# A second table of turns, engines and buffer slots for the same 1,612 operations of an attention and long-convolution kernel

## The chip, the cores and the metric

One Trainium2 chip, one core. The metric is the time of one execution on the device in microseconds; the median of three runs stands for the kernel.

## The reference, cut to what matters

Two independent halves write the left and the right 576 columns of one output of 2048 rows.

```python
# A: 32 heads of 18, 4 segments of 512 rows, with a memory carried from segment to segment
q, k, v = x @ wq, x @ wk, x @ wv
for s in range(4):
    p = softmax(qs @ ks.T * scale + causal_mask)          # 512 x 512 for each head
    a_mem = (phi(qs) @ M) / (phi(qs) @ z + 1e-6)          # phi(t) = t+1 if t>0 else exp(t)
    o = g * a_mem + (1 - g) * (p @ vs)
    M, z = M + phi(ks).T @ vs, z + phi(ks).sum()
a = concat(o) @ wo
# B: a short filter of 4 taps, a product, a convolution over all 2048 rows by FFT, a product
kv = short_filter(k, shift_k) * v
y = irfft(rfft(kv) * rfft(ssm_k))[:2048] + kv * ssm_D
b = q * y
out = concatenate([a, b])
```

## The kernel before

The kernel builds a graph of 1,612 operations and then emits them in one written order. An operation is a small group of instructions on one engine: five matmuls into one PSUM tile, the copy of that tile to SBUF, one DMA. `ORDER` is that order. Each operation has three characters in it: two digits to the base of 64 give its number in the graph, and a letter gives its engine (P TensorE, A ScalarE, D VectorE, G GpSimd, S the queue of SyncE, which issues every DMA). Each engine runs its own operations strictly in this order, and a DMA whose data is not ready holds up all DMAs behind it. `PLACES` gives each of 1,039 buffers its slot; a slot is used again only when the last reader of the buffer before has ended. PSUM has eight banks (`ps1` takes one, `ps2` two).

```python
for i in range(0, len(order), 3):
    o = g.ops[64 * code[order[i]] + code[order[i + 1]]]
    o.eng = {"P": "PE", "A": "ACT", "D": "DVE", "G": "POOL", "S": "SP"}[order[i + 2]]
...
for o in order:
    o.fn(o.eng)
```

Half A, for each segment `s` (lines from 780 on): `x` loads five transposed tiles of the input (`xT`, L800); `qk` and `v` project them (PE, L150), `qkp` does so for the first two groups of heads of segment 0 in another layout; the copies `eqk`, `ev` go to `dn` and `V`; `qd` writes q and k to a scratch in DRAM and `pad` reads them back with each head on 32 partitions; `s0`, `s1`, `s2` are the scores of four heads in three pieces (PE, L1046), each followed by two exponentials of 128x1024 on ACT (`exs`, L1053) and a mask on POOL (`m`, L1060); `av` multiplies by V (L152), `eav` copies it, `ad` writes it to DRAM, `cs` and `am` read sums and rows back, `rs`, `rx`, `rsb`, `o` normalise, `num` and `oo` add the memory's part, `out` is the last projection, `eout` its copy, `oA` its store. `phe`, `phm`, `pha` make phi (exponential on ACT L889, maximum, minimum), and `tk` transposes it by DMA.

Half B, for five groups of 128 (the last 64) channels: `kT`, `vT` load k and v transposed (L374, L377), `dg` makes diagonal weights, `conv` is the short filter (PE), `kv` its product with v (DVE L404), `tinx` a 32x32 transpose (DVE L416); `xsh` loads the long filter, `dadd` adds D to it (needs the DMA `Dt`, L350); `F1x`, `F1h`, `F2x`, `F2h` are the two stages of a Fourier transform as matmuls (L152) with copies; `Q`, `P`, `Yi`, `Yr` multiply the spectra (DVE or POOL); `inv`, the transposing DMA `zt`, and `last` transform back; `y` multiplies by q; `yo` stores.

The tables of the Fourier transform are made on the chip: `iota` (POOL), `idx` (DVE, L288 and L290), `sin` (ACT, L295) for four quarters of `Ft`, and `w1iota`, `w1idx`, `w1sin`, `w1mask` for `W1`; `gT` (PE) and `g` turn `Ft` over for the inverse, `psie`, `psiT`, `psi` make a small matrix from `W1`. `beta` loads the gate, `gexp` takes its exponential (ACT L664). The sine and the exponential are in different activation tables, so each change from one to the other on ACT brings an ACT_TABLE_LOAD. Copies on ACT bring none.

Of the kernel before, what the change touches and what calls it, by code (L numbers as in the profile page):

```python
# [18 lines left out]
S = 2048  # L19
# [103 lines left out]
class Prog:  # L123
# [1159 lines left out]


ORDER = (
    "0RG00G01D06G09D0ZS0WS0-S0+S11S0VG0qG0YG0vG0zS10S0mG0oG0XS0aS0US0bG0wG0AA02G03D0pD1MD0cS14P1CP18P0tS0dS1wP16P1yP12P0rS"
    "0yS0TS0hS04A19A0iSGoS0xSGpS0SS0jS1RG15A1kAGqG1UP28PGvP17A07D1xD13D1zD1DA08A1hA0gS05G0BG1oD0ED26P1APGtP1PPGrP1iD1jD1VD"
    "29D2AS0FA0kA0CD0DA1nA27A0fSGuD1BDGWSGwD1WSGsDGxPGyDGzD1XSIDS1QA1SP22P23A0nG0GGIiGGXD1pD1TD0PP0LP0NP1lG1NPICS0QA0OAGkP"
    "GiPGaP1OAGlA0MA20P24P25AGjAGbD1mD2BSGePGgPGmPGhDH4PHAPGYPH8PGnAGcPH0PHBAGZAH1A21AH5DGfD2CSIOSIgS0sS1bS1YSG+PHCPH6PH9A"
    "GdD1+PG-DH7DHDDHkPHiPHEPHVPH2PHGP1KPHHDHlAH3AHWAHTPHZPHjAHaDHXPHKPHxP1LAHYA1tAHyAHLAI1P0HPHIPHUDHbG1uD0IDHJD1vDHFAHMD"  # L1290
    "HcDIPD1GP1EPI2D1HA1qA1FA1-A1IP2QPIaPISPIcP1JA2SAHmPIbD4bS4aS4dS4cS4ZSHnAIWPIePH-P1aS2ESIhS1cSIdDITDI0AIXA0JPIQPIUPHzP"
    "HdG1rG0KD1sDIYP2RAH+AIRAIfDIVD2TGHND2IPHoPHpDHqDHrDHODIjPIZAHtDHPD2JA2KA2XP4gP2YA2ZA2aG2MPHsD0lD2NA2OA5dPHeG4hD5eA4eP"
    "JcP4fD5DD2LG2bP5fP59A5CAJdD5gD5ED4iP4jD2dA2cA2PGKGS2eG4yS0uS1ZS1dS2DSIkD5JD5IA5KD5ADIlP2qP2rA2sAHQPHRDImDHSDJNPHfP2fP"
    "HhDI3GI5G5BDKHDI4DJOA2iPHgAHuP2UPHvDI6D2kA2VA2gAIpPHwA2jAInPIqDIoDI7PI8DI9A2xPIBSIAS2yAIrD2zA4kP2mPJ6P2WS1gS1eS2oA2nA"
# [45 lines left out]


# [63 lines left out]
```

## Time and profile before

| | us |
|---|---|
| three runs | 342.86, 340.09, 337.14 |
| median | 340.09 |
| the profiled execution | 341.92 |
| its span, first to last instruction | 340.2 |

| engine | busy us | share of the span |
|---|---|---|
| PE | 285.5 | 84% |
| DVE | 266.1 | 78% |
| ACT | 258.6 | 76% |
| POOL | 181.3 | 53% |

Busy times of PE come from modelled ends of pipelined matmuls. The mean granted clock of PE is 0.909 of full speed.

### The profile page before, as it was taken

The page shows a single profiled execution, that of the slowest core. Times are in us where ns is not written, and L with a number is a line of the kernel's source. Part 1 is how long each engine was busy: PE and PEld are TensorE (multiplying, and loading weights), DVE is VectorE, ACT ScalarE, POOL GpSimd, SP SyncE. Part 2 cuts the span into 40 slices and gives each one's busy share as a digit, 9 for nine tenths or more (in the row PEclk, how much of TensorE's full clock was granted, in tenths as well). Part 3 has the DMA queues.
Part 4 walks back from the last instruction along what each step waited for, and adds up shares of the span by engine and source line. Part 5 has one row for each costly group of instructions (what it writes and reads, how often), then busy time and mean ns, then how long its engine had stood idle before and what let it go on. Part 6 is the DMA issues. An engine that isn't in the chain of part 4 may idle for free.

```text
span 340.2 us, 8802 instructions
## 1 busy us (share of the span) xinstructions
PE 285.5 (84%) x3515; PEld 163.9 (48%) x3515; DVE 266.1 (78%) x454; ACT 258.6 (76%) x362; POOL 181.3 (53%) x228
## 2 busy tenths in 40 slices
PE   0886998889979868889998999989895788997776
PEld 0453575444744446444555556546453254453334
DVE  6557477898999998969889998889969965655670
ACT  2197787987977869837999986888689569879813
POOL 8694007282785975654437423794858742435600
PEclk9999799997998979959999999999998559579969
DMA  8687489791996964776689687757359347453204
GB/s 199 172 178 104 108 111 161 136 176 33 212 175 182 167 154 89 160 139 184 136 180 151 156 166 149 148 144 180 85 129 195 88 94 166 96 140 102 80 17 101
DMA packets 119011, 47.13 MB, mean 139 GB/s; under 512 B 101946, under 2 KB 112570, under 8 KB 118970
## 3 DMA queue, kind: packets, MB, share of 16 engines
q1 hardware_dynamic: 118970, 46.58, 67.1%
q8 instruction: 27, 0.44, 0.5%
q14 instruction: 14, 0.11, 0.1%
HBM read 17.74 MB, written 14.42 MB: 95 GB/s over the span
## 4 chain that ended last, share of the span: by engine, by line
PE 36%; DVE 25%; ACT 12%; DMA 9%; issue 6%; SPq 6%; POOL 4%; DVEq 0%; ACTq 0%; POOLq 0%
PE PS L150 20%; PE PS L152 12%; ACT P L1053 8%; PE PS L1046 4%; DVE A L158 4%; DMA a_scratch<-ou 3%; DMA pad<-qk_scratch 2%; DVE X L158 2%; SPq L800 2%; DVE T L520 2%; DMA Dt<-in_A_beta_dram 2%; DMA q<-in_B_q_dram 2%; DVE H L524 2%; DVE X L404 2%; DVE H L158 1%
## 5 line engine op out<-in xcount | busy, mean ns | idle before, releaser
L1053 ACT ACTIVATE P<-PS 128x1024 bf16<-128x1024 f32 x160 | 154.7, 1036 | 28.6 <-PE PS L1046 25.4
L1060 POOL TENSOR_SCALAR_AFFINE_SELECT P<-P 128x512 bf16<-128x512 bf16 (+1 forms) x112 | 81.0, 744 | 86.0 <-ACT P L1053 55.2
L1046 PE MATMUL PS<-pad 18*128 18x384 bf16 (+3 forms) x512 | 39.9, 323 | 12.9 <-ACT P L1053 5.9
L158 DVE CAST A<-PS 128x512 bf16<-128x512 f32 (+1 forms) x64 | 41.4, 680 | 9.6 <-PE PS L152 9.4
L150 PE MATMUL PS<-xT,wk 128*126 128x512 bf16 (+1 forms) x100 | 28.5, 423 | 11.1 <-DMA xT<-in_A_x_dram 9.6
L152 PEld LDWEIGHTS <-Ft 128*64 128x64 bf16 x704 | 24.7, 113 | 15.4 <-issue 11.7
L520 POOL TENSOR_TENSOR T<-X,H 128x512 bf16<-128x512 bf16 x16 | 20.0, 1271 | 21.4 <-DVE H L158 19.8
L156 ACT CAST A<-PS 128x512 bf16<-128x512 f32 (+1 forms) x48 | 26.8, 601 | 5.8 <-PE PS L152 5.7
L1046 PEld LDWEIGHTS <-pad 18*128 18x128 bf16 x512 | 12.4, 93 | 37.6 <-issue 33.7
L152 PE MATMUL PS<-P,V 128*32 128x256 bf16 (+3 forms) x512 | 26.2, 333 | 3.4 <-DVE A L158 1.7
L152 PE MATMUL PS<-W,xs 128*64 128x128 bf16 (+1 forms) x608 | 24.4, 225 | 5.0 <-DVE ou L158 1.6
L152 PE MATMUL PS<-A,Ft 128*64 128x128 bf16 (+1 forms) x640 | 25.8, 218 | 3.3 <-DVE ou L158 1.9
L150 PE MATMUL PS<-wo,am 126*128 126x288 bf16 (+1 forms) x152 | 26.6, 312 | 0.9 <-DVE am L1215 0.5
L152 PEld LDWEIGHTS <-xs 128*64 128x64 bf16 (+1 forms) x608 | 19.9, 114 | 12.4 <-issue 9.7
L150 PE MATMUL PS<-xT,wq 128*126 128x512 bf16 (+1 forms) x100 | 25.0, 382 | 0.0
L150 PE MATMUL PS<-wv,xT 128*128 128x288 bf16 x160 | 24.3, 294 | 0.5 <-ACT P L1053 0.5
L150 PEld LDWEIGHTS <-wk 128*126 128x126 bf16 (+1 forms) x100 | 13.5, 144 | 20.9 <-issue 8.5
L150 PE MATMUL PS<-X,dg 128*128 128x512 bf16 x80 | 21.6, 404 | 0.9 <-DMA X<-in_B_k_dram 0.9
L152 PEld LDWEIGHTS <-V 128*32 128x32 bf16 x512 | 12.4, 103 | 18.2 <-issue 9.2
L150 PEld LDWEIGHTS <-am 126*128 126x128 bf16 (+1 forms) x152 | 14.7, 105 | 9.8 <-issue 3.5
L158 DVE CAST dn<-PS 126x512 bf16<-126x512 f32 (+1 forms) x22 | 14.9, 682 | 5.4 <-PE PS L150 4.4
L150 PEld LDWEIGHTS <-xT 128*128 128x128 bf16 x160 | 15.1, 101 | 8.1 <-issue 3.0
(164 smaller groups left out, 555.4 us busy)
## 6 DMA issues: line engine op xcount, KB each, us to landing
pad<-qk_scratch SPq DMA_DIRECT2D x30, 256.0 KB
qk_scratch<-dn SPq DMA_DIRECT2D x16, 252.0 KB
a_scratch<-ou SPq DMA_DIRECT2D x31, 128.0 KB
out_dram<-oA SPq DMA_DIRECT2D x16, 144.0 KB
xs<-in_B_ssm_k_dram SPq DMA_DIRECT2D x4, 512.0 KB
q<-in_B_q_dram SPq DMA_DIRECT2D x8, 256.0 KB
out_dram<-q SPq DMA_DIRECT2D x8, 256.0 KB
am<-a_scratch SPq DMA_DIRECT2D x16, 126.0 KB
```

The lines of the kernel that those rows point to most:

```text
L150: self.nc.tensor.matmul(out, lhsT=lhsT, rhs=rhs, start=start, stop=stop)
L152: self.nc.tensor.matmul(out, lhsT=lhsT, rhs=rhs, start=start, stop=stop, tile_position=pos)
L156: self.nc.scalar.copy(out=out, in_=in_)
L158: self.nc.vector.tensor_copy(out=out, in_=in_)
L404: self.nc.vector.tensor_tensor(out=v, in0=self.psf(pc)[lo:P, :], in1=v, op=ALU.mult)
L520: eng.tensor_tensor(out=t[:, 512 * r:512 * r + 512], in0=x[:, 512 * r:512 * r + 512], in1=h[:, 512 - 512 * r:1024 - 512 * r], op=ALU.mult)
L524: eng.tensor_tensor(out=self.t(Ht)[:], in0=self.t(Xt)[:], in1=self.t(Ht)[:], op=ALU.mult)
L800: self.nc.sync.dma_start_transpose(out=self.t(b)[:], in_=self.A_x[0, L * s:L * s + L, c0:c0 + P])
L1046: nc.tensor.matmul(o, lhsT=t[r, 1, q0:q0 + P], rhs=t[r, 0, q0:L], start=True, stop=True, tile_position=(32 * j, 0))
L1053: self.nc.scalar.activation(out=out2(jj), in_=self.psf(pso[jj]), func=ACT.Exp, scale=scale)
L1060: self.nc.gpsimd.affine_select(out=ap, in_=ap, compare_op=ALU.is_ge, fill=0.0, base=0, pattern=pat + [[1, P]], channel_multiplier=-1)
```

## The change

The operations, their code and the buffers' sizes stay. `ORDER` and `PLACES` are replaced as a whole, so turns, engines and slots are new.

```diff
 ORDER = (
-    "0RG00G01D06G09D0ZS0WS0-S0+S11S0VG0qG0YG0vG0zS10S0mG0oG0XS0aS0US0bG0wG0AA02G03D0pD1MD0cS14P1CP18P0tS0dS1wP16P1yP12P0rS"
...
+    "0YG00G01D0oG02G0pD03D0cS0+S0-S11S10S0bG0qG06G04A05G0VG0RG0GG0HP07D08A0ID09D0BG0wG0zS0dS0ZS0iS0aS0US0XS0WS0TS1MG1RG0vG"
...
 PLACES = (
-    "101101164624031042600221314025504101221072312301101101100503132020610042646402635142546230602040461004650431160520424"
...
+    "010010006462040132703014021724115123121011203210100101001110630224006002450402432004404271060642061000454632146264406"
...
```

Read back into names, the first turns of each queue are these:

```
ACT before  sin01 w1sin eqk eqk phe eqk eqk sin00 phe sin11 gexp sin10 phe ev eqkp ev g10 g11 ...
ACT after   w1sin sin00 sin01 ev sin10 eqk phe eqk sin11 phe gexp eqk g10 g11 phe ev ...
DVE before  cols idx01 w1idx cmask wp0 idx00 ev eqk ev phm idx11 phm pha eqkp ev idx10 kv0.1 ...
DVE after   cols cmask w1idx idx00 psi idx01 idx10 dg0 ev ev idx11 phm eqk eqk pha eqk kv0.3 ...
SP  before  wk wq x(5) wq4 wk4 sk4 wv wop wv4 wop fz1 sk beta beta kT0 fz0 vT0 Dt beta2 beta tk wo4 xsh0 ...
SP  after   wv x(5) wv4 wk beta wk4 sk4 wq4 wq sk wop kT0 beta2 vT0 beta wop beta xsh0 tk Dt fz1 qd fz0 ...
PE  before  qk x3, v, qk, v, qk, qkp, v, conv, v, qk, conv, qkp, conv x2, qkp, v, gT x3, qkp, F1 ...
PE  after   psiT, v x3, qk x5, conv x4, qk, gT x3, v, qkp, F1 ...
```

Ahead of the first `F1`, PE has 6 `qk`, 5 `v`, 4 `qkp`, 4 `conv` and 3 `gT` in the table before, and 6, 4, 1, 4 and 3 and the small `psiT` in the new one.

About 200 operations change their engine. Of the copies out of PSUM 78 go from ACT to DVE and 71 from DVE to ACT: 57 and 61 of 512 columns, 20 and 10 of 288, and one of 1024 to DVE. Between DVE and POOL: `Q` 5 to DVE and 4 to POOL, `P` 3 and 2, `Yi` 5 and 3, `Yr` 5 and 7, `phm` 5 and 7, and one or two each of `dg`, `dx`, `rx`, `wp`. PE and SP have the operations they had. The 80 score operations stand in the same order but for exchanges of near neighbours, and from the last `inv` of group 3 to `last3` lie 15 operations of PE in the old table and 17 in the new.

## Rows read from the trace of the kernel before

**Rows 1.** Stages: PE, PEld, DVE, ACT, POOL busy; clock, DMA share, GB/s.
```profile
0.00:35.00 35.00, 21.46 (x101) 11.53 (x103) 23.28 (x46) 18.76 (x22) 24.66 (x58) 1.00 0.76 166
35.00:255.00 220.00, 197.39 (x2730) 118.03 (x2727) 190.46 (x321) 180.31 (x269) 120.92 (x124) 0.95 0.74 146
255.00:302.00 47.00, 38.72 (x425) 20.08 (x420) 33.27 (x55) 36.36 (x42) 25.23 (x31) 0.64 0.58 126
```

**Rows 2.** Instructions of PE in order of time, 0 to 45 us: start, us.
```profile
11.97 4.33 PE L150 MATMUL PS<-xT,wk 128*126 128x512 bf16 x11 [0.82 <-DMA wk<-in_A_wk_dram]
...
22.25 1.03 PE L150 MATMUL PS<-X,dg 128*128 128x512 bf16 x4 [0.87 <-DMA X<-in_B_k_dram]
23.11 0.78 PE L150 MATMUL PS<-wv,xT 128*128 128x288 bf16 x5
23.73 1.24 PE L150 MATMUL PS<-xT,wq 128*126 128x512 bf16 x5
...
35.71 3.70 PE L152 MATMUL PS<-ident,Ft 128*64 128x128 bf16 x32 [0.29 <-ACT V L156]
...
40.56 0.86 PE L152 MATMUL PS<-W,xs 128*64 128x128 bf16 x24
```

**Rows 3.** Instructions of ACT in order of time, 0 to 60 us: start, us.
```profile
22.70 1.28 ACT L889 ACT_TABLE_LOAD   x1
24.00 0.63 ACT L889 ACTIVATE fk<-dn 126x512 bf16<-126x512 bf16 x1
...
29.47 1.28 ACT L664 ACT_TABLE_LOAD   x1 [2.48 <-DMA Dt<-in_A_beta_dram]
...
32.37 1.06 ACT L295 ACTIVATE Ft<-xs 128x1024 bf16<-128x1024 int32 x1
```

**Rows 4.** The DMA queue of SP, 0 to 45 us: start, time to issue.
```profile
1.86 6.99 SPq L800 DMA_TRANSPOSE xT<-in_A_x_dram  x5
...
9.54 0.58 SPq L623 DMA_DIRECT2D wk<-in_A_wk_dram  x1
...
15.62 3.82 SPq L374 DMA_TRANSPOSE X<-in_B_k_dram  x1
...
20.11 2.84 SPq L377 DMA_TRANSPOSE X<-in_B_v_dram  x1
...
23.66 2.10 SPq L659 DMA_DIRECT2D Dt<-in_A_beta_dram  x1
25.82 0.63 SPq L646 DMA_DIRECT2D Dt<-in_A_beta_dram  x1
```

**Rows 5.** Instructions of DVE in order of time, 0 to 60 us: start, us.
```profile
4.56 2.77 DVE L290 TENSOR_SCALAR xs<-xs 128x1024 int32<-128x1024 int32 x1
...
28.16 0.69 DVE L290 TENSOR_SCALAR xs<-xs 128x1024 int32<-128x1024 int32 x1
...
33.46 2.11 DVE L416 STREAM_TRANSPOSE xs<-X 128x1024 f32<-128x1024 f32 x1 [1.62 <-ACT Ft L295]
```

**Rows 6.** Groups of instructions by line, shapes apart, the whole span.
```profile
L158 DVE CAST X<-PS 128x512 bf16<-128x512 f32 x21 | 14.1, 685 | 3.9 <-PE PS L152 2.5 <-ACT dn L156 1.1 <-ACT V L156 0.2
...
L156 ACT CAST oA<-PS 128x288 bf16<-128x288 f32 x20 | 8.1, 416 | 11.9 <-PE PS L150 10.4 <-DMA out_dram<-oA 1.3
```

**Rows 7.** What PE waited for, 255 to 302 us: total, times, longest.
```profile
PE PS L152 <- DMA A<-A: 1.2, 1, 1.2
```

**Rows 8.** PE in two stretches: busy, instructions, clock, DMA share, GB/s.
```profile
250.00:260.00 10.00, 8.08 (x205) 1.00 0.85 157
260.00:270.00 10.00, 6.19 (x66) 0.57 0.54 118
```

**Rows 9.** The exponentials (L1053 on ACT) late: busy, count, clock, DMA share, GB/s.
```profile
283.00:322.00 39.00, 33.50 (x36) 0.82 0.48 117
```

**Rows 10.** The chain that ended last, from 311 us on: start, us.
```profile
318.87 3.19 DMA a_scratch<-ou
...
329.51 7.48 PE PS L150 x45
```

More of the change, by code (lines that the diff above doesn't have):

```diff
@@ new lines @@
+    "GbAH7AHBAH5AHDAGiPGjD1XSIgS2CS0uSH2PGmPH0PH8PGYPGgPIOS1bSGnD1jD2AS1cSH1AG-A28P1NPH3A29AH9DGePHKPHXPI1PHIPHJDHLDGZAICS"
+    "IDS1WS0sS1SP24PHYDGfAGhA1OA0lD20PI2A1TA25AHZPHxPHEPHkPHGPHTPHaAHyDH-PHzPHFDHlDI0AHHDHMD1GPH+AHNDI3D1PP1HAHUAIPD1qA1rD"
+    "HPG1KP1QA1LA1uD1sDHVPHWAI4DHbGI5DI6DHmPHOGHdGHnA1tA1EPHcG2QP1FA2RA1IP1+P2SA1-AIQPIWPISP21D1JDIXDIRAIUPIcPIePIdD0JPIVA"
+    "IfAITAHoP0KD2XPHiPIaP2YA2ZAHpDHjDHQPIYP2IPIbD1vDIZDHRAHSA1ZS2KA2JAHeDHqDHrDHsDIpPIjPHtD2MP2NA2OA4cS4aS4bS4dS4ZS2PG2LG"
@@ new lines @@
+    "2aGJ6P4ePIhSJ7D5fP4fD5DD5gA2bP2dAJcP4iP2cA5CA4jA5IA2ES1eSKGS2DS4gP2TGIkDIqDJdD2qPHfP4hD5JD5EDHhD2UP2VDHgD1aS1dS4yS2WS"
+    "0fSInPIoD2rA2sA59AKHD5KDJpP2iPJqA0mG5AG2jAIlP2kA4kP4lAKaG2eG2tG5GGImDIrD5BD2xPJrPHuPHwDHvD4mP2zA5FA2yAI7P4nAI8AI9DJsD"
+    "5PGIwPIyPJNPJ0PIsPJ2PIxDJ4P5HDJ3DIuPIvDJ5D2lG2+GIzAItAJOAJ1AJ8P5OAJ9AJLP2fPI+P4oP5QD4pDI-AJCPJvPJtPJMA2gA2mPJDAJwAJuD"
+    "JxDJyD5MD5dPIBS2FPIAS2GD2HD2oA2nAJeP2-P5eAIGP2pG2hSIIPIJDKYSJfA30A31A32GKUPJAPKMPKOPKSP64S65SIHDIKPJzGKPDKVAKNAKZS4+S"
@@ new lines @@
+    "KQPJPPKWPKIPJRPILDJBAJ+GKTAJSAJQDJgPJaPIEPKJDJbD5LA5NDIFDKRAKXA4sP4tA5RAJhD5SD5TDJEDJFDJTGJUDIMSJHDINS4zS1gSJWG4qP4rA"
+    "2uP66S2vA33P34A3AP3BAJVG67SJGG2wS40S35S1fSK5S3wSK4SKbPKdP3CA5UAKcD5VDKeD5WD3EP3GAKfPKhP3FA3DG36P3HG37A38A39GKgDKiDKjD"
+    "KKP4uPKLAJXP3LPLFP4vAJiGJjGJkGJYAJlGJZDLGDKwPKsPKqPKoP5bDKrD3NA3MAK+PKyP3IPKkPL0PKpDK-DKzDKlDKxAKtA5aA3JAL1A5cD4wP3PP"
+    "4xD50S43S3KS3OGMSGKuPKvD54S51SJIP3QA3RAJKD3aPKmPJmP3xDKnD5YD3bA3cAJ-PL2PJoDJnAJJDL3AL4PLDP3WP3SG3yG5XAK1AL5D3TPK0D5ZD"
@@ new lines @@
+    "K3S3UD3VSK2S3dGL6G46SMQSLJPLKD41P44P42D45D3YA3XA68S3ePLUPLEA3gA3fA3hGLVDL7DLjPLkD3ZG3lP3mA3nAL9G3oG5tP3pP5uDLWP3rA3qA"
+    "3iPLYPLXD5vDLnPLoDLZA3sG6GP6HA6IA62P3jDLHPK8PLSPKAP63DLTA3tP3kSK9DKBD3uA6CP6DA52S6EALIA3vS5hP5wPMRS5lP5jPLaDLbD5nP5kA"
+    "5iD5xD5oD5mAKCPK6P6JGLLG6KPKDD3zSK7DL8DLMD3+D0eS49S4CS5rP5pPMTP60P5qD61D53S6LA8dS8fS8hS8eS8gS5sA6MA3-G6RPMXPMUDMYDMZP"
+    "47P6TA6SA6VPKFSM8SKES4-S6XA6WA6FG6UG55S6NGLdG6YG69P48DMaD6AD5+P4DPMVP6gP4ED5yP4AP6hA6iAMWD5-D4BD6BD5zD6OP6ZP6PA6cP4FP"
@@ new lines @@
+    "4KP8iP6aA6eA6dAMbD6jGLNG4MP4HP6bS58S6QS4LA8jA9GA6vP6xA6wA4IA6yG4GD4NDLlPMqP8oP9HD9IDMrD6fG8pD9KD9JALmA9LDA9SLzS9hP9iD"
+    "M9D6kP8mP8nD8kP6lA6mA56S6rP4OS4JS8lDMAPMgPLhP6sAMBDLiDLOD6tA6nGMhAOCD9ED6uG8sP6oP8tA9DA6pDLAPLCD70PMMPMND8qP6zP8rDLBD"
+    "71A72A9PA90S74PLPP4WP6+DLQD4XDLRD9FD76A75A6qS6-SOAS7qS7wS9jP9kDLcGLpGLqD57S73GLrD77GLsD78P79A7AA8uP7FP7HA7GA9QD8vD9RD"
+    "8wP4PP7BG9NG91SA8S4QDMIPMkPMJD7JP4RP4UP8xAMlD7rD9WD4VD4SD7LA7KA7-S7IG7sG7MGMCP7CPMDA7DD7UP7xPMiP7WA7VA7zP7yD7+DLePMjD"
@@ new lines @@
+    "LgDLfAOBS9VA9MA7NP7QP95S96S7ES9XDABS80P82P8+P81D83D9TD8-DLtP7OA7RA7SALvDLuD9SAMKPMeP7YP9OD9cDMfD7ZA7aA7XG7TG7bG7PSLxS"
+    "84SAASLwS8yPOJP7fPOFP9UD8zDOKD9fGOGDMLA7hA7gA9bAOHPOID7jP7iG7cP7lA7kA7mG9dD7dDMoPMGPMEPMmPMOP7eSMHAMPAMpDMnDMcPLySODP"
+    "MdAMFDAGP7nPOED7oDACS7pS89SO0S7tS8ES4YS92SN9P9pP9rP9nP9qDAHAAIANAA9oAAKPALA9sDOLD9tP87P9lP9eAAMA9uDM2PM4PNfPM5DMuPNKP"
+    "MsPM0PNgANLAMvA9vP9mDM3D9gDM1D7uD9ZGAJGANG7vG8CPN5PL+PMwP9wA9YACkSChSClSCjSCiS9aDL-DM6S97S98S93SADPAEDMxAO1DMtAN6A9xP"
@@ L1339 @@
+    "175141006001113703312010617204075050265164060703232711235327102067403125145100306072302164501072460602701354240122054"
+    "062121511261320116753201120110413714334530270103232042431210762542205423037112232410071575102210273064741310107325010"
+    "4057060646247623672221233000061633214260740401152671002261724050107672070426614421276067135203123012032"
 )
```

71 lines of the change are left out of this document (22 added, 49 removed).

## The prediction

> **What bounds the kernel now.** The order of reading was: busy time by stage, then in the worst stages each queue in order of time, then the chain that ended last.
>
> The stages differ [rows 1]. From 35 to 255 us PE is busy for 197.39 of 220 us at a clock of 0.95, with DVE at 190 and ACT at 180: three engines are near their limit, and a new order can win there only from the 22.6 us in which PE stands idle. In the first 35 us PE is busy for 21.46: 13.5 us are lost to loads and tables. From 255 to 302 us PE is busy for 38.72 of 47, but at a mean clock of 0.64. That is 38.72 x 0.36 = 13.9 us of clock lost, and it begins where PE had been busy for 8.08 and then 6.19 of 10 us [rows 8]. The clock has two levels, 1.2 and 2.4 GHz, so 0.57 means mostly the lower one. From 283 us on ACT carries the end: its exponentials alone take 33.5 of 39 us [rows 9]. After the last of them comes a fixed chain: a store of 3.19 us, a load, some products, and 7.48 us of matmuls [rows 10].
>
> So there are four places where a new table can move the end: the head, the waits of the middle, the low clock before 283 us, and the tail. Work moved between engines is not one of them, as the next paragraphs show.
>
> **Engine totals.** ACT gets 4 more copies of 512 columns than it loses and loses 10 of 288 and one of 1024. With 0.416 us for 288 columns [rows 6] and estimates from it, 0.6 for 512 and 1.1 for 1024, that is 2.4 - 4.2 - 1.1 = -2.9 us. DVE gets about as much at 0.685 for 512 [rows 6], +3, and some products to and from POOL which nearly cancel. Against 190 and 180 us busy in 220 this is one per cent, spread over the span. I take 0, and ±1.5 us for the end.
>
> **The head.** Here the order is different enough to be followed step by step, to the first F1, which starts at 40.56 us now [rows 2].
>
> Loads. The SP queue issues wv, five transposed loads (6.99 us [rows 4]) and wv4 first, until about 8.8 us. The last weight piece now ends its issue at 9.54 + 0.58 = 10.12 and its matmul goes on at 11.97 [rows 2, 4], so a landing takes 1.85 us: `v` starts at 10.7. Three `v` follow at 0.62 each (23.11 to 23.73 [rows 2]) and end at 12.6. wk4 is issued by 10.6 and lands by 12.5. Three `qk` (1.24 each [rows 2]) end at 16.3, and two more with wq at 18.8.
>
> `conv` waits for kT0. Its issue takes 3.82 us and its matmul ran 2.8 us after the end of that (15.62 + 3.82 to 22.25 [rows 2, 4]). In the new queue two loads and small pieces stand ahead of it, it is issued from 13.3 to 17.1, and `conv` starts at 19.9 instead of 22.25. Four `conv` (0.86 each, 22.25 to 23.11 [rows 2]) and a `qk` end at 24.6.
>
> `gT` needs the sines. Now ACT changes its table eight times, and four sines end at 32.37 + 1.06 = 33.43 [rows 3], with a wait of 2.48 us for the gate in front of the last. In the new order three sines come first and the fourth after one exponential: two tables of each kind, four loads instead of eight, 4 x 1.28 = 5.1 us less. The sines share one slot with their indices, so they run one after the other: an index takes 1.4 to 3.8 us on DVE (two passes: the second 0.69 to 2.77 [rows 5], the first estimated at 0.7 to 1), a sine 1.06 on ACT [rows 3]. From w1sin at 7.1 I get 10.6, 14.4, 17.9 and, after `dg0` and two copies on DVE and a table load, 22. All are ahead of 24.6, so PE does not wait. The table loads are thus worth their time only as far as they release `gT`; they are not a term of their own.
>
> Rows 3 show the ACTIVATE 0.02 us after the end of a load of 1.28. The Trainium skill, ScalarE: Activation LUTs, "What ACT_TABLE_LOAD costs", puts a switch at about 2.66 us, with a drain beside the load. By that the four would free 10.6 us of ACT instead of 5.1; the trace has no room for the drain.
>
> Three `gT` took 3.70 us for two, so I take 5 us with the third: 29.6. One `v` and one `qkp` (0.62 and 1.24) bring F1 to 31.5. Its other inputs: vT0 is issued by 22.0 (2.10 for the gate's broadcast ahead of it, 2.84 itself [rows 4]), lands at 24.9, four products of 0.68 and a transpose of 2.11 [rows 5] end at 29.7. Dt, moved behind `tk` on SP, which waits for `pha` on DVE at about 23, is issued by 26 and in SBUF by 29 (3.0 us, as the gate's: 26.45 to 29.47 [rows 3, 4]); `dadd` then takes 0.3 to 0.5. Both are within 31.5. Moving `gexp` ahead of the copies on ACT costs nothing while the gate, issued by 23.9, lands by 27: the copies behind it wait for `gT` anyway.
>
> F1 is earlier by 9.1 us. But one `v` and three `qkp` that stood ahead of it now stand behind, 0.62 + 3 x 1.2 = 4.2 us [rows 2]. The head gains 4.9 us. From above, with 1.2 us for each `gT`, 6.3. From below 0: PE is 90% busy behind the head, but a later wait for the exponentials or a pad could give all of it back.
>
> **New waits in the head.** `psi` now stands fifth on DVE, ahead of the second index. It waits for w1sin, two masks and small writes on POOL (3 us together) and a matmul; the first index (1.5 to 3.8 us) runs meanwhile. Bounds 0 and 1.5 us for the sines, which have 2.7 us or more of cover. `dg0` moves from POOL to DVE behind three index pairs, and `conv` waits for it. DVE has no row of this operation; I bound it by one copy of 512 columns, 0.69, and one transpose of 1024, 2.11 [rows 5, 6], and take 1.2, which ends it at about 18, 1.9 us ahead of kT0.
>
> **The middle and the low clock.** The 80 scores are in the same order but for neighbours, so this is a reworked table and not a different plan. Counted in PE operations, transfers have the cover that they had or a little more. One of them ended a wait of PE in the late stage, A<-A with 1.2 us [rows 7]; 17 operations instead of 15 cover it in the new table. I take -1 us. The other waits in the 22.6 us of idle PE [rows 1] are single and of many kinds: a sixth of them more or less, -4 to +4 us, taken as 0. The low clock is taken as it is.
>
> **The tail.** The copy `enm` of 512 columns (0.6 us) no longer stands ahead of the last `eav` but one on ACT, and the stores of group 4 of half B leave the last turns of SP. The fixed chain stays. -0.5 us, between 0 and -1.2.
>
> **The sum.** 341.92 - 4.9 - 1.0 - 0.5 = 335.5 for the profiled execution's own time. That execution is 1.83 us above the median, 340.09, so against the runs it is 333.7 us. From no change a measurement of this kernel can tell about 2%, 6.8 us; the forecast is 1.9% below and nearly on that bound.
>
> **The rivals.**
>
> *The clock holds.* If PE comes to 250 us with the head's lead and without the two slices of 8.08 and 6.19, the lower clock of 260 to 283 goes. Price: 6.19 x 0.43 = 2.7 us for the first ten [rows 8], and about as much again for the next thirteen, with waits -6: 327.7. For it: the fall came after short waits which a redraw may move. Against it: from 283 on ACT sets the end [rows 9], so nothing can be won behind it, and DVE has as much to do there as before.
>
> *The head's lead is lost.* Then only the tail and a wait remain: 338.6. It decides if the indices run slowly: the same instruction took 2.77 us at 4.56 and 0.69 at 28.16 [rows 5], and in the new order three pairs run ahead of `dg0` while POOL writes its constants. With 1.4 us more for each pair `dg0` ends at 22.2, `conv` starts 2.3 us later, and the head gains 2.6: 336.0. With a wait for the exponentials behind it, 339. The Trainium skill, SBUF — State Buffer, "Who interferes with whom", says that VectorE and GpSimd share a pair of ports by an exclusive lock; the two rows agree with it in kind.
>
> *A second fall of the clock (slower).* The stretch of 35 to 255 us runs at 0.95 because waits are short. If the new order opens one gap there like that at 260, twenty microseconds at 0.55 with 15 busy cost 15 x 0.45 = 6.8 us, and the waits themselves 5: 333.7 + 11.8 = 345.5. [...] The place would be where SP, in order, stands before a DMA whose data is not ready while x or a pad is queued behind it. Against it: the covers are not shorter.
>
> **How the numbers follow.** Forecast, 330 to 338: 0.44. The clock holds, 323 to 330: 0.24. The lead is lost, 336 to 341: 0.18. A second fall, 341 to 350: 0.14. The range of 8 in 10 takes in the first three and the near half of the last: 325 to 344. Below 333.3 us lie the second case and half of the forecast, 0.45; above 346.9 the far part of the last, 0.09, and I give 0.12 for what a table of this length can hide; 0.43 remain.
>
> **What would show it.** Four ACT_TABLE_LOADs. First F1 at 30 to 33 us, `conv` at 20. The clock of 255 to 302 us near 0.64, and the last exponential 18 to 19 us ahead of the end. A wait of over 2 us on PE behind the head, or a stretch at the lower clock ahead of 250 us, would make the forecast wrong.

## The result and the profile after

The new table takes 314.25 us (median of 4 runs, 312.06 to 318.47) against 338.62 for the old one (4 runs). The ratio is 0.928 with a 95% interval of 0.917 to 0.938. The forecast was 333.7 us, 325 to 344, so the result lies below the range. The profiled execution took 313.88 us, with a span of 312.2 us and a mean clock of 0.956 instead of 0.909. (Executions of one kernel differ by some per cent with the granted clock, so times below are medians of all of them, ratios compare the faster ones alone, and for six kernels (old turns with new engines, more on ACT, the two with other slots, the head with its own slots, the products alone in another form) the profiled execution was one of the longer ones, by 1.6 to 3.7%.)

To see where 28.0 us of span went, the two kernels are compared at equal work of PE. Each matmul is priced at its duration at the full clock, and the stage bounds are the moments at which the sum passes 40, 112, 240 and 276 us (about 311 in all). In the old kernel these are 57.1, 131.1, 249.2 and 293.2 us, in the new one 51.7, 113.5, 227.3 and 263.7. A bound is good to about 1 us.

| us | to work 40 | 40 to 112 | 112 to 240 | 240 to 276 | to the end | span |
|---|---|---|---|---|---|---|
| old | 57.1 | 74.1 | 118.1 | 44.0 | 47.0 | 340.2 |
| new | 51.7 | 61.8 | 113.8 | 36.5 | 48.5 | 312.2 |
| gain | 5.4 | 12.3 | 4.3 | 7.5 | -1.5 | 28.0 |
| predicted | 4.9 | 0 | 0 | 1.0 | 0.5 | 6.4 |

The head's gain came near its forecast. What was missed lies behind it: 24 us between work 40 and 276, of which 1 was counted. The table is from one trace of each kernel. In six traces of kernels below that have the old turns on the old engines from work 240 to 276, this stage takes 41.4 to 45.1 us; in six that have the new ones it takes 37.2 to 38.4. The 7.5 us there are thus at the upper end.

The stages that answer to [rows 1], in the new kernel (window, its length, then PE, PEld, DVE, ACT, POOL busy with their instructions; clock, DMA share, GB/s):

```profile
0.00:35.00 35.00, 23.44 (x187) 14.07 (x191) 24.99 (x50) 17.11 (x24) 25.28 (x53) 1.00 0.79 166
35.00:227.30 192.30, 178.83 (x2536) 107.77 (x2540) 175.31 (x314) 169.44 (x251) 118.33 (x128) 1.00 0.89 165
227.30:274.00 46.70, 40.90 (x537) 21.15 (x536) 35.50 (x63) 42.36 (x51) 26.69 (x32) 0.84 0.66 148
```

In the long middle PE now stands idle for 13.5 of 192 us instead of 22.6 of 220, and the clock is 1.00 instead of 0.95. The late stage runs at 0.84 instead of 0.64.

PE's head and one stretch of ACT's, which answer to [rows 2] and [rows 3] (start, us):

```profile
11.14 0.40 PE L150 MATMUL PS<-ident,Pe 32*128 32x32 bf16 x2 [11.14 <-POOL Pe L310]
11.85 3.76 PE L150 MATMUL PS<-wv,xT 128*128 128x288 bf16 x15 [0.31 <-DVE Psi L323]
...
21.28 3.62 PE L150 MATMUL PS<-X,dg 128*128 128x512 bf16 x15
24.74 1.24 PE L150 MATMUL PS<-xT,wq 128*126 128x512 bf16 x5
25.91 5.46 PE L152 MATMUL PS<-ident,Ft 128*64 128x128 bf16 x48
...
33.11 3.89 PE L152 MATMUL PS<-W,xs 128*64 128x128 bf16 x120
```

```profile
21.91 1.28 ACT L295 ACT_TABLE_LOAD   x1
23.21 1.06 ACT L295 ACTIVATE Ft<-xs 128x1024 bf16<-128x1024 int32 x1
24.29 1.28 ACT L889 ACT_TABLE_LOAD   x1
```

The last of four sines ends at 24.27 us, `gT` starts at 25.91 and F1 at 33.11 instead of 40.56.

Now the middle. These are the three stages between work 40 and 276, first of the old kernel, then of the new one, in the columns of the fence on stages:

```profile
57.10:131.10 74.00, 62.74 (x910) 38.04 (x905) 68.56 (x109) 61.12 (x89) 46.40 (x48) 0.93 0.82 148
131.10:249.20 118.10, 109.09 (x1372) 62.72 (x1371) 104.99 (x181) 96.35 (x140) 66.51 (x71) 0.97 0.70 150
249.20:293.20 44.00, 35.22 (x476) 18.78 (x474) 31.51 (x51) 35.55 (x43) 24.11 (x29) 0.72 0.65 142
```

```profile
51.70:113.50 61.80, 57.09 (x923) 34.88 (x926) 59.30 (x104) 58.58 (x90) 47.57 (x54) 1.00 0.90 164
113.50:227.30 113.80, 105.21 (x1380) 62.09 (x1377) 102.29 (x186) 96.69 (x135) 66.71 (x73) 1.00 0.85 169
227.30:263.70 36.40, 31.20 (x451) 16.30 (x451) 29.20 (x52) 33.92 (x42) 23.76 (x28) 0.91 0.74 157
```

The engine to look at is DVE. In the first of these stages of the old kernel it is busy for 68.56 of 74.0 us: it is the busiest engine there, more than PE with 62.74. In the new kernel the same stage of PE's work holds 9.3 us less of DVE, but only 5 instructions fewer. So the single instruction has become shorter. These are DVE's groups by line over the whole span (count; busy us, mean ns of one), of the old kernel and then of the new one:

```profile
L520 DVE TENSOR_TENSOR T<-X,H 128x512 bf16<-128x512 bf16 x20 | 12.6, 667 | 0.2
L524 DVE TENSOR_TENSOR H<-X,H 128x1024 bf16<-128x1024 bf16 x13 | 12.1, 932 | 1.1 <-POOL T L520 1.0
L534 DVE TENSOR_TENSOR H<-H 128x512 bf16<-128x512 bf16 x10 | 6.0, 608 | 0.1
...
L158 DVE CAST A<-PS 128x512 bf16<-128x512 f32 x57 | 36.8, 680 | 7.6 <-PE PS L152 7.4
```

```profile
L520 DVE TENSOR_TENSOR T<-X,H 128x512 bf16<-128x512 bf16 x22 | 10.5, 518 | 0.2
L524 DVE TENSOR_TENSOR H<-X,H 128x1024 bf16<-128x1024 bf16 x14 | 9.8, 708 | 0.2
L534 DVE TENSOR_TENSOR H<-H 128x512 bf16<-128x512 bf16 x8 | 4.2, 522 | 0.1
...
L158 DVE CAST A<-PS 128x512 bf16<-128x512 f32 x55 | 35.8, 678 | 1.5 <-PE PS L152 1.3 <-ACT oA L156 0.2
```

The same product with both inputs in SBUF takes 667 ns in one kernel and 518 in the other; a copy out of PSUM takes 680 and 678. Set against POOL's spans, 10 of the 20 products T<-X,H of the old kernel have POOL busy for over 60% of their time and take 920 ns on average, and 9 have it idle and take 415; in the new kernel 5 of 22 have it busy, and 17 idle (857 and 418). The reason is seen where two engines are laid side by side. In the old kernel, the product `xf` on DVE and what POOL did (start, us):

```profile
116.50 2.51 DVE L1172 TENSOR_TENSOR xf<-rb,m 128x512 bf16<-128x512 bf16 x1
```

```profile
116.33 2.12 POOL L524 TENSOR_TENSOR H<-X,H 128x1024 bf16<-128x1024 bf16 x1
118.41 1.92 POOL L1060 TENSOR_SCALAR_AFFINE_SELECT P<-P 128x512 bf16<-128x512 bf16 x2
```

POOL began a product of 2.12 us at 116.33, and DVE's, issued 0.17 us later, ended only after it, at 119.01. In the new kernel this `xf` runs on POOL. Whether this waiting is the cause of the lost time, or only goes with a worse order, is what the experiments had to settle.

The late stage and the end, which answer to [rows 7 to 10]: PE's wait for A<-A went from 1.2 to 0.9 us (total, times, longest):

```profile
PE PS L152 <- DMA A<-A: 0.9, 1, 0.9
```

The clock fell in the new kernel too, but for a shorter time. These are stretches of the new kernel, then of the old one:

```profile
237.00:242.00 5.00, 3.43 (x40) 1.51 (x41) 4.93 (x9) 3.86 (x5) 4.04 (x5) 0.62 0.69 205
242.00:247.00 5.00, 4.76 (x48) 1.75 (x44) 4.77 (x8) 4.48 (x6) 3.40 (x5) 0.69 0.31 102
247.00:252.00 5.00, 4.69 (x97) 2.94 (x97) 4.09 (x7) 4.91 (x7) 1.87 (x3) 1.00 0.83 182
```

```profile
260.00:265.00 5.00, 2.29 (x26) 1.07 (x26) 4.90 (x7) 3.08 (x4) 5.00 (x6) 0.63 0.89 211
265.00:270.00 5.00, 3.89 (x40) 1.67 (x43) 4.87 (x8) 3.38 (x4) 4.80 (x5) 0.50 0.18 26
270.00:275.00 5.00, 4.39 (x63) 2.54 (x56) 2.86 (x6) 4.14 (x5) 1.64 (x3) 0.50 0.47 124
```

The old kernel had PE busy for 2.29 and 3.89 of 5 us around the fall, with DVE (4.90, 4.87) and POOL (5.00, 4.80) both full; the new one lost less there, and PE was busy for 4.76 when the clock came back. The last exponential ends at 292.76 us, 19.4 ahead of the end:

```profile
289.90 2.86 ACT L1053 ACTIVATE P<-PS 128x1024 bf16<-128x1024 f32 x3
```

### The profile page after: what moved, and what is told of

Its sections match the earlier page's. It is cut to its first block, busy times and chain, and to the rows that moved or that the text cites. A ratio compares the mean times of both kernels' runs of the same rounds, so it can differ in the third digit from the quotient of the medians.

```text
span 312.2 us, 8836 instructions
## 1 busy us (share of the span) xinstructions
PE 272.5 (87%) x3504; PEld 157.6 (50%) x3515; DVE 255.6 (82%) x460; ACT 249.9 (80%) x351; POOL 181.6 (58%) x229
## 5 line engine op out<-in xcount | busy, mean ns | idle before, releaser
L1053 ACT ACTIVATE P<-PS 128x1024 bf16<-128x1024 f32 x160 | 154.2, 1035 | 20.2 <-PE PS L1046 16.1
L1060 POOL TENSOR_SCALAR_AFFINE_SELECT P<-P 128x512 bf16<-128x512 bf16 (+1 forms) x112 | 79.0, 724 | 64.7 <-ACT P L1053 46.1
L1046 PE MATMUL PS<-pad 18*128 18x256 bf16 (+3 forms) x512 | 41.9, 311 | 7.6 <-ACT P L1053 4.1
L158 DVE CAST A<-PS 128x512 bf16<-128x512 f32 (+1 forms) x62 | 40.2, 678 | 2.4 <-PE PS L152 2.2
L152 PEld LDWEIGHTS <-Ft 128*64 128x64 bf16 x704 | 23.3, 111 | 11.3 <-issue 7.3
L534 POOL TENSOR_TENSOR H<-H 128x512 bf16<-128x512 bf16 x10 | 12.6, 1263 | 24.0 <-DVE H L524 24.0
L152 PE MATMUL PS<-P,V 128*32 128x256 bf16 (+3 forms) x512 | 24.0, 315 | 1.6 <-POOL P L1060 0.4
L150 PE MATMUL PS<-xT,wk 128*126 128x512 bf16 (+1 forms) x100 | 25.4, 388 | 0.0
L150 PEld LDWEIGHTS <-am 126*128 126x128 bf16 (+1 forms) x152 | 15.6, 109 | 11.1 <-issue 4.2
L150 PE MATMUL PS<-X,dg 128*128 128x512 bf16 x72 | 19.2, 380 | 1.6 <-DVE X L404 0.5
L520 POOL TENSOR_TENSOR T<-X,H 128x512 bf16<-128x512 bf16 x14 | 17.8, 1291 | 2.4 <-ACT X L156 2.0
L158 DVE CAST oA<-PS 128x288 bf16<-128x288 f32 x20 | 9.0, 454 | 11.5 <-PE PS L150 9.7
```

The source lines that it names most:

```text
L150: self.nc.tensor.matmul(out, lhsT=lhsT, rhs=rhs, start=start, stop=stop)
L152: self.nc.tensor.matmul(out, lhsT=lhsT, rhs=rhs, start=start, stop=stop, tile_position=pos)
L158: self.nc.vector.tensor_copy(out=out, in_=in_)
L520: eng.tensor_tensor(out=t[:, 512 * r:512 * r + 512], in0=x[:, 512 * r:512 * r + 512], in1=h[:, 512 - 512 * r:1024 - 512 * r], op=ALU.mult)
L534: eng.tensor_tensor(out=t[:, 0:512], in0=t[:, 512:1024], in1=t[:, 0:512], op=ALU.subtract)
L1046: nc.tensor.matmul(o, lhsT=t[r, 1, q0:q0 + P], rhs=t[r, 0, q0:L], start=True, stop=True, tile_position=(32 * j, 0))
```

## The experiments

"Old" and "new" are the two tables. Ratios are to the old kernel on the same chip, with a 95% interval; the new kernel's is 0.928. All other code is unchanged.

### Turns, engines and slots, each by itself

```diff
-order, engines, slots = old, old, old
+order, engines, slots = new, old, new        # new turns, old engines
+order, engines, slots = old, new, old        # old turns, new engines
+order, engines, slots = old, old, mixed      # other slots: 288 of 1,039 buffers, all first used in turns 1 to 600
+order, engines, slots = old, old, mixed_psum # the same for PSUM alone: 185 buffers
```

New turns, old engines. 

> The turns and slots of the new table, with every operation on the engine that it has in the old one (about 200 operations go back, among ACT, DVE and POOL). Theory 'turns': the order alone closes the waits of the middle, so this runs in 314 to 320 us. Rival 'engines': the gain behind the head comes from what DVE and POOL do beside each other (DVE's instructions took 11.0 us less in sum at the same count); with the old engines DVE is back at 264 to 267 us busy and the time is 328 to 334 us, that is, only the head's 5.4 us and a few more remain. The mean of the DVE product T<-X,H, 667 ns with the old table and 518 with the new, should stay near 520 by the first and go back to 650 or more by the second.

Old turns, new engines. 

> The turns and slots of the old table, with the new engines. By 'turns' this is no faster than the old kernel: 335 to 342 us, T<-X,H near 650 ns. By 'engines' it has the gain of the middle without the head: 319 to 328 us, T<-X,H near 520 ns. If both tables are only good as a whole (engines were drawn together with turns), both this and the crossed kernel beside it are over 330.

Other slots. 

> The old turns on the old engines; only the slots differ: buffers that are first used in the first 600 turns take the new table's slot where it is free in the order of turns, 288 of 1,039 differ (185 of them in PSUM). Theory from the kernel with the old turns to 132 us, which ran the same turns on the same engines 35 us slower in that stretch: slots are part of a table as much as turns, since a tile waits for the last reader of its slot, and this is 360 us or more. Rival: slots are a matter of names, and what was slow there was something else: 335 to 342 us.

Other slots in PSUM. 

> The old turns and engines with other slots as before, but for PSUM alone (185 buffers); all tiles in SBUF keep theirs. If the banks are what the turns were fitted to, 375 us or more of the 391; if it is the slots in SBUF, which hold up DMAs in SP's queue (one stood 12.2 us for a reader in DVE), 340 to 355.

Measured: 387.5 us (ratio 1.143, 1.135 to 1.150), 397.3 (389.0 to 403.3), 391.4 (1.139, 1.123 to 1.156) and 377.0 (1.109, 1.091 to 1.128). Both theories of the first pair were wrong, and its third case came true far beyond its number: one part of a table without the others costs 37 to 57 us, some twice what the whole change gains. The sign that was named for the two theories, the mean of T<-X,H, came to 561 and 613 ns, between the 518 and 667 of the two tables, and decides nothing. The stage of work 40 to 112 takes 103.8 us in the new turns with the old engines, against 74.1 and 61.8 in the two whole tables. So the parts can't be credited with shares of the gain. Where the time goes is seen in SP's queue of the kernel with other slots, from 44 to 170 us (total, times, longest):

```profile
SPq L984 <- DVE fk L903: 17.8, 2, 12.2
SPq L566 <- DVE A L158: 14.4, 2, 11.7
SPq L1141 <- DVE ou L158: 11.5, 2, 9.7
```

A DMA stands for a tile that DVE has not yet made or read, and all DMAs behind it wait. In the old kernel the same three waits come to 8.8, 9.3 and 7.0 us up to 131 us. DVE in turn waits for PE: its copies to A alone for 28.0 us in this stretch. That PE waits for a bank would fit; no row here shows it. With the banks alone changed, the stage of work 40 to 112 is as slow as with all (104.2 and 104.3 us), so the banks are enough for it.

### Splices: is a stretch's time its own?

```diff
-order = old
+order = new[:140] + rest of old      # head, old slots where free
+order = new[:105] + rest of old      # head, each turn with its own table's slots
+order = old[:240] + rest of new      # old head, new slots where free
+order = old[:600] + rest of new      # old to 132 us, new slots where free
+order = new[:1245] + rest of old     # new to 228 us, own slots
+order = new[:1440] + rest of old     # new to 265 us, own slots
```

Engines go with the turn. Head, first try. 

> The first 140 turns of the new table (up to the first F1) with their engines, then all that is left in the old order on the old engines. If the head is a term by itself, as the prediction has it, the first F1 starts at 32 to 34 us and the end is 4 to 6 us earlier: 333 to 335 us. If the lead is lost behind the head, 337 to 340. If the lead is what opens the rest (operations start before DVE's crowded stretch), 325 or less.

Head with its own slots. 

> The first 105 turns of the new table (to 33 us, up to the first F1) with their engines and slots, then all that is left in the old order, with the old slots but one. The head alone, without the foreign slots of the first try. If the head is a term by itself: 333 to 335 us. If the lead is given back behind it: 338 to 341.

Old head. 

> The first 240 turns of the old table (to 62 us in the old kernel, where the new one is 5 to 6 us ahead), then all that is left in the new order on the new engines. If head and middle add up, this is the new kernel plus 5 to 6 us: 319 to 321 us. If the later gain hangs on the head's lead, 328 or more.

Old to 132 us. 

> The first 600 turns of the old table (to 132 us in the old kernel), then all that is left in the new order on the new engines. The head's 5 us and the 12 us of 57 to 131 us are given up. If what the new table gains behind that (11 us in the traces, of which some by a higher clock) is its own, the end is at 326 to 330 us. If it only follows from the earlier start, 336 to 341.

New to 228 us. 

> The first 1,245 turns of the new table (to 228 us in the new kernel, 22 us ahead of the old one at the same work), then what is left in the old order, 5 slots changed. If the last 6 us of gain (250 to 285 us of the old kernel, where the clock was 0.71 and is 0.88) belong to the new turns there: 319 to 322 us. If the clock recovered because PE comes there with less idle time behind it: 313 to 317.

New, then the old tail. 

> The first 1,440 turns of the new table (to 265 us), then what is left in the old order, 10 slots changed. At the same work the old last stretch took 42.4 to 43.8 us in five traces, the new one's 43.4 to 44.9 in three: if that is the tables' own, 313 to 314 us; if not, 314 to 316.

Measured: 343.8 us (1.008, 1.003 to 1.014), 337.5 (0.980, 0.970 to 0.991), 333.2 (0.980, 0.973 to 0.987), 370.6 (1.091, 1.082 to 1.100), 321.1 (0.945, 0.938 to 0.952) and 316.1 (0.933, 0.917 to 0.949).

The first head lost its lead between work 20 (36.7 us, 4.0 ahead) and work 40 (60.5, 3.4 behind), in the 20 us behind the joint; the second kept its 3.9 us at work 40 (53.2 us) and was faster by 2%. The two differ in the place of the joint and in foreign slots, which these runs don't separate. The two with old turns on new slots point to the slots: they lost 7 and 8 us before work 40 and, with 600 such turns, 35 us by work 112, where their turns and engines are the old kernel's. These two thus say little of what they were made for; by its expectation alone, 333.2 us would have spoken for a later gain that hangs on the head's lead, and 370.6 lies beyond both cases. One reading of the third run holds: it came to work 48 18 us behind the new kernel and took 113.7 us from work 112 to 240 (new 113.8) and 37.8 from 240 to 276 (new 36.5). There the stretches behind the joint take their table's time, whatever the start, and nothing is made up.

The fifth says the same of the late stage. It runs at the new pace to 228.0 us (work 240) and then on the old turns:

```profile
228.00:273.00 45.00, 35.65 (x449) 18.84 (x450) 32.57 (x52) 34.52 (x42) 25.55 (x29) 0.72 0.58 129
```

It takes 45.1 us from work 240 to 276, as the old kernel does (44.0), at a clock of 0.72, though it came there 21 us earlier and at the full clock. The low clock is not inherited; it comes back with the old turns. The last splice can't be told from the new kernel.

### A microsecond more on each engine

```diff
     for k, o in enumerate(order):       # the new tables
         o.fn(o.eng)
+        if k in at:   # 35 places, or 22, or 14, between 52 and 107 us; a tile that no one reads
+            nc.vector.tensor_tensor(out=xb[:], in0=xa, in1=xa, op=ALU.mult)   # or scalar.copy, or gpsimd.tensor_tensor
```

More on DVE. 

> The new kernel with 35 small products (128x256, no one waits for them) added on DVE between 52 and about 107 us; estimated at 0.2 to 0.3 us each, 7 to 10 us together. Theory: from 52 to 113 us DVE (59.3 us busy of 61.8) sets the pace, and the middle gained because DVE had 9.3 us less to do there than in the old kernel (68.6 of 74.0). Then the added time comes out at the end nearly whole: 320 to 324 us. Rival: PE and the transfers set the pace, and DVE was only busy beside them: under 317 us.

More on ACT. 

> The same with 22 copies of 128x256 on ACT in the same stretch, estimated at 0.35 to 0.45 us each, 8 to 10 us together. ACT is busy for 58.6 of 61.8 us there, so it has 3.2 us to take them in. If ACT is as near to the limit as DVE, the end is 5 to 7 us later, 319 to 322. If the exponentials have slack against PE and only DVE counts, under 317.

More on POOL. 

> The same with 14 products of 128x256 on POOL in the same stretch, estimated at 0.6 to 0.7 us each, 8 to 10 us together. POOL is busy for 47.6 of 61.8 us there and could take them. If work of POOL makes DVE's products from SBUF longer (T<-X,H on DVE: 415 ns beside an idle POOL, 860 to 920 beside a busy one), DVE's busy time in the stretch grows by 2 to 5 us and the end with it: 317 to 321. If DVE and POOL don't touch each other, 314 to 316.

Measured: 329.1 us (0.971, 0.962 to 0.980), 320.0 (0.936, 0.928 to 0.944) and 317.3 (0.937, 0.930 to 0.945). At the end only the first is clear of the new kernel's own 0.928 (0.917 to 0.938). From work 40 to 112 the stage grew by 15.6, 5.1 and 5.0 us for 19.1, 10.9 and 8.8 us added, in one trace of each and with a clock of 0.93, 0.98 and 0.95 instead of 1.00. DVE passes on 0.8 of a microsecond. For ACT and POOL it is about half by these traces, which the times at the end don't confirm. POOL had 14 us to spare, and its work should have cost by making DVE's instructions longer; DVE was busy for some 2 us more in the stage, but so it was with the work on ACT, so this path isn't shown. An addition tells what more work on DVE costs in the new kernel, not what less would give: that is the last experiment.

The added products cost twice what was estimated, 547 ns instead of 200 to 300, and they are a measurement by themselves. All 35 are alike:

```profile
L1379 DVE TENSOR_TENSOR extra<-ident 128x256 bf16<-128x256 bf16 x35 | 19.1, 547 | 0.0
```

In order of time on DVE, and POOL beside them:

```profile
79.29 0.28 DVE L1379 TENSOR_TENSOR extra<-ident 128x256 bf16<-128x256 bf16 x1
...
102.70 1.24 DVE L1379 TENSOR_TENSOR extra<-ident 128x256 bf16<-128x256 bf16 x1
...
105.03 1.23 DVE L1379 TENSOR_TENSOR extra<-ident 128x256 bf16<-128x256 bf16 x1
```

```profile
78.69 1.92 POOL L898 TENSOR_SCALAR fr<-dn 126x512 bf16<-126x512 bf16 x1 [2.16 <-ACT dn L156]
...
102.53 1.26 POOL L534 TENSOR_TENSOR H<-H 128x512 bf16<-128x512 bf16 x1 [5.08 <-DVE H L524]
103.76 2.35 POOL L529 TENSOR_TENSOR T<-T 128x512 bf16<-128x512 bf16 x2
```

The one at 102.70 met a product that POOL had begun at 102.53, and ended 0.15 us after it. The one at 79.29 ran in 0.28 us beside an operation of POOL of 1.92 us; that one has one input and scalars.

### Relieving DVE in the old kernel by seven engines

```diff
-engines: eqk1.10 eqk1.11 eqk1.20 eqk1.31 eF1h2.4 eZ1.4 on DVE, rx0.0 (xf) on DVE
+engines: eqk1.10 eqk1.11 eqk1.20 eqk1.31 eF1h2.4 eZ1.4 on ACT, rx0.0 (xf) on POOL
```

> The old turns and slots; of the engines only seven change, all between 66 and 118 us: six copies of 512 columns from DVE to ACT and one product of 2.5 us (xf) from DVE to POOL. DVE gets 6 x 0.68 + 2.5 = 6.6 us less to do, in a stretch where it is busy for 68.6 of 74 us; ACT gets 3.6 us more, of 12.9 that it has. If DVE's busy time sets the pace there: 332 to 335 us. If each copy's place in its engine's order matters more, as the crossed kernels suggest: 338 or more.

Measured: 338.2 us (0.996, 0.991 to 1.000). From work 40 to 112 the stage takes 72.2 us instead of 74.1:

```profile
56.90:129.10 72.20, 59.85 (x910) 36.25 (x905) 63.48 (x102) 63.69 (x95) 46.59 (x49) 0.98 0.84 154
```

DVE has 5.1 us less in it and the stage gains 1.9, so the theory as stated failed. ACT now has as much to do as DVE (63.69 us), which would explain it: moving work between them wins little, and the sum has to fall. The rival, that each copy's place in its engine's order counts, is not excluded.

### The waiting beside POOL, taken out

POOL's products and masks are replaced by its operation of one input on fewer columns, so that each takes about as long. The second factor, a part of the columns and the causal mask are left out; three memsets, 2.8 us on POOL, are added to the kernels in which the products are replaced.

```diff
-eng.tensor_tensor(out=t[:, 0:512], in0=t[:, 0:512], in1=t[:, 512:1024], op=ALU.add)        # on POOL; DVE keeps it
+gpsimd.tensor_scalar(out=t[:, 0:300], in0=t[:, 512:812], scalar1=-3.0e38, scalar2=0.0, op0=ALU.max, op1=ALU.add)
-gpsimd.affine_select(out=ap, in_=ap, compare_op=ALU.is_ge, ...)                             # [128, 4, 128]
+gpsimd.tensor_scalar(out=ap[:, :, 0:40], in0=ap[:, :, 0:40], scalar1=-3.0e38, scalar2=0.0, op0=ALU.max, op1=ALU.add)
```

In the old kernel. 

> The old kernel; on POOL alone the products and the masks are replaced by a scalar operation of one input (maximum with -3e38, plus 0) on fewer columns, 300 for 512, 552 for 1024 and 160 for a mask of 512, so that each takes about the time that it took; beside that operation on POOL (L898) DVE's products took 251 to 281 ns in the kernel with more on DVE, and 560 to 1240 beside POOL's products and masks. It leaves out the second factor, the rest of the columns and the causal mask, so that its output is another. Theory: DVE's instructions lose their 35 us of waiting beside POOL to 5 to 15, DVE is not the pace any more, and the time falls to 320 to 329 us. Rival, DVE's waiting is covered by waits that it has anyway: 335 to 341.

In the new kernel. 

> The same replacement in the new kernel, which leaves out the same parts. DVE waits 23 us beside POOL here, 12 less than in the old kernel. If these 12 us are the middle's gain, the time falls by 3 to 8 us (306 to 311), and the gap to the old kernel with the same replacement is 10 to 16 us instead of 24. If they are not, the gap stays over 20.

Masks alone, in the old kernel. 

> The old kernel with only the masks of POOL as the scalar operation (the causal mask is left out); its products stay. Of POOL's 46 us in 57 to 131 us the masks are 19.4 and the products 24. If each kind holds DVE up in proportion to its time, this gives about 45% of the 17 us: 329 to 333 us. If only products of two inputs hold DVE up: 337 to 340. If only masks do: 320 to 324.

Products alone, in the old kernel. 

> The old kernel with only POOL's products as the scalar operation (their second factor and part of the columns are left out); the masks stay. In proportion: 328 to 332 us. If only products hold DVE up: 320 to 324. If only masks do: 337 to 340.

| | us | ratio | DVE busy | POOL busy |
|---|---|---|---|---|
| old | 338.6 | 1 | 266.1 | 181.3 |
| old, both | 320.95 | 0.953 (0.942 to 0.965) | 246.0 | 194.7 |
| new | 314.25 | 0.928 (0.917 to 0.938) | 255.6 | 181.6 |
| new, both | 314.13 | 0.937 (0.925 to 0.949) | 245.5 | 198.6 |
| old, masks | 334.06 | 0.982 (0.975 to 0.990) | 260.0 | 194.4 |
| old, products | 321.58 | 0.944 (0.933 to 0.954) | 250.2 | 181.6 |

With POOL busy 13 us longer, the old kernel is 16 to 17 us faster, as its first theory had it. The new kernel gains nothing, where 3 to 8 us were expected, though DVE is busy for 10 us less in it: relieved of this waiting, it has another limit. The gap of 24 us between them shrinks to 7 (10 to 16 were expected), which is the head and a little, and the difference of 10.5 us in DVE's busy time shrinks to 0.5. The old kernel with both replaced, stage by stage:

```profile
55.20:120.10 64.90, 58.47 (x910) 35.92 (x908) 59.80 (x109) 61.44 (x90) 50.98 (x50) 1.00 0.92 173
120.10:233.60 113.50, 105.48 (x1367) 60.98 (x1371) 96.25 (x181) 95.86 (x140) 69.41 (x70) 1.00 0.78 158
233.60:270.10 36.50, 30.52 (x476) 17.06 (x475) 28.03 (x51) 35.22 (x43) 26.93 (x30) 0.89 0.65 151
```

It takes 64.9, 113.5 and 36.5 us where the old kernel takes 74.1, 118.1 and 44.0 and the new one 61.8, 113.8 and 36.5. The same 109 DVE instructions of the first stage take 59.80 us instead of 68.56, and the low clock of the last one, 0.72, is 0.89. Over the span its products T<-X,H take 456 ns on average instead of 667, not yet the 415 beside an idle POOL: of 48 products of DVE that began beside the new form, 16 were still lengthened, all 48 together by 2.9 us.

```profile
L528 DVE TENSOR_TENSOR T<-X,H 128x512 bf16<-128x512 bf16 x20 | 8.3, 456 | 0.2
```

A replaced product no longer reads its second factor, so it could also start too early. It did in two of eight cases with the products alone replaced, by 0.40 and 0.03 us; that is not where 17 us come from.

Of the two kinds the products do nearly all: alone they give 5.6%, the masks 1.8%. The products came out as if they alone held DVE up, the masks between two of their cases. Together they give no more than the products alone. In the first stage ACT is then busier than DVE (61.44 against 59.80 us), which fits. The clock of the late stage is another matter: it takes 38.9 us at 0.76 with the products alone and 41.2 at 0.77 with the masks alone, so the higher clock came only with both, and in one trace.

Two things stay open. In the second stage the old kernel gains 4.6 us with 8.7 us less on DVE, the new table 4.3 with 2.7 less: the waiting is enough to explain it, but that the new table gains there by the same means is not shown. And in the first stage 3 us remain between the old kernel with both replaced and the new one. ACT is busy for 2.9 us less there in the new one (58.58 against 61.44), which would fit; no run tests it.

## Why the prediction was wrong

**The head: right in its steps, near in its sum partly by luck.** Forecast a gain of 4.9 us, found 5.4 at work 40, and 2% (0.9 to 3.0) in the splice with its own slots. Four table loads, each 1.28 us. `conv` came at 21.28 instead of 20 and F1 at 33.11 instead of 31.5: PE stood until 11.14 us for POOL's `Pe`, since `psiT` is the first turn of PE. Under "New waits in the head" `psi` was priced for DVE and `psiT` not for PE. The last sine came at 24.27 instead of 22, still ahead of `gT`. So F1 was 7.5 us earlier and not 9.1; less the 4.2 us of work put behind it this is 3.3, and some 2 us more were won between F1 and work 40, which the forecast had not counted.

**Engine totals: the step that failed.** It says that DVE gets 3 us more and that "work moved between engines is not one of" the places where a table can win. The count was right: at the old mean durations DVE's new list costs some 2 us more. But it took an instruction's duration for a constant. DVE's busy time fell by 10.5 us, because the new table puts fewer of its products from SBUF beside a busy POOL. ACT's fell by 8.7 us, and there the count was nearly all: 2.9 for the copies and 5.1 for four table loads. The two rows that hint at DVE's waiting were quoted (L290 at 2.77 and 0.69 us), but only as a risk for the head. The groups by line would have shown it for the whole kernel: T<-X,H has a mean of 667 ns, and those beside an idle POOL take 415.

**The middle: the same cause, shown for the first stage.** Its other waits were taken as 0 with bounds of 4 us; the stages gave 12.3 + 4.3. "A new order can win there only from the 22.6 us in which PE stands idle" was too narrow as well: the stage ran at a clock of 0.95 on 197.39 busy us, which is 9.9 us more to win. With most of the waiting beside POOL taken out, the old turns give 9.2 of the 12.3 and as much as the 4.3. The remaining 3 us of the first stage belong to something else in the new table, which no run here takes apart.

**The low clock: taken as it is, and wrong.** It gave 7.5 us instead of 1.0. The rival that the clock holds had this sign, but its price (2.7 us for ten, as much again, waits of 6) and its reason (the head's lead) were not what happened: the spliced kernel with all of the lead had the low clock back, and the old turns lost most of it when both kinds of POOL's operations were replaced. A<-A, the wait that I named, changed by 0.3 us.

**The tail:** -0.5 forecast, +1.5 found. The last 45 matmuls take 8.87 us instead of 7.48 [rows 10], at a granted clock of 0.65 instead of 0.77: the chain that was called fixed is not. The last exponential is 19.4 us ahead of the end, against 18 to 19.

**A second fall of the clock** did not come.

## What to carry to other kernels

Before a schedule is changed, group the instructions of each busy engine by shape: where one shape's mean is far above its shortest, as 667 against 415 ns here, the time can be waiting inside the instruction, which counts as busy and stands in no list of waits. Ask what the other engines run at that time; here it was POOL. And a table of turns, engines and slots is one object: a part of another good table in it can cost more than the table gained.

## What was not expected of the hardware

- DVE's 128x256 product took 275 to 285 ns beside an idle POOL and up to 1240 beside a product or mask of POOL; the wait is inside the instruction. The Trainium skill, SBUF — State Buffer, "Who interferes with whom", says that a VectorE instruction with two SBUF inputs contends with a GpSimd instruction that reads SBUF. The traces agree for POOL's products and masks: of DVE's products with both inputs in SBUF that began while a product of POOL ran, 80% of 289 in all traces were lengthened by over 0.1 us (against the median of their shape beside an idle POOL), on average by 0.62; beside a mask 77% of 269, by 0.34. For POOL's operation of one input with scalars they agree only in part: it reads SBUF for 1.9 us, DVE's products ran to their end beside it in 0.25 to 0.28 us, and of 172 such meetings 27% were lengthened, all together by 0.07 us on average and at most by 0.45. On this weaker hold the replacement above rests. DVE's copies out of PSUM were not touched: of 1,276 that began beside a product or mask of POOL none took over 16 ns more.
- A wait on DVE can cost in two ways, as idle time of PE and by its clock: the stage of work 240 to 276 of the old turns became 7.5 us shorter when most of DVE's waiting was taken out, and in this PE's busy time, for the same 476 matmuls, fell from 35.22 to 30.52 us at a clock of 0.89 instead of 0.72. This is one trace against one; the old turns alone take 41.4 to 45.1 us here.
- Slots alone, with the same turns and engines, made the kernel slower by 14%; PSUM banks alone by 11%.
